# A linear-attention and Fourier-filter kernel on one core: new set-up of the DFT tables, half transposes of q and k, and another order on every engine

## The chip, the core and the metric

The kernel runs on one core of a Trainium2 chip. A core has five engines, each with an instruction queue of its own that is worked off in order: TensorE (PE in the profile; PEld is its weight load), VectorE (DVE), ScalarE (ACT), GpSimd (POOL) and SyncE (SP), which here only issues DMAs. DMAs are issued by SP and POOL and carried out by the core's 16 DMA engines. The metric is the device time of one execution in microseconds (us), lower is better.

## The reference

The inputs are q, k and v (8 batches, 8 heads, 576 positions, 64 wide), a feature map w_phi (64 x 128), a projection w_proj (512 x 1536), a filter (576 x 512) and w_out (512 x 512), all in float32.

```python
def phi(x):
    proj = einsum('bhsd,df->bhsf', x, w_phi)
    proj = proj - max(abs(proj), axis=-1, keepdims=True)
    return concatenate([exp(proj), exp(-proj)], axis=-1)
q_p, k_p = phi(q), phi(k)
kv  = einsum('bhsf,bhsd->bhfd', k_p, v)
z   = sum(k_p, axis=2)
num = einsum('bhsf,bhfd->bhsd', q_p, kv)
den = einsum('bhsf,bhf->bhs', q_p, z)[..., None] + 1e-06
x   = (num / den).transpose(0, 2, 1, 3).reshape(8, 576, 512)

x1, x2, x3 = split(x @ w_proj, 3)
conv = irfft(rfft(x2, axis=1) * rfft(filter_fft, axis=0), n=576, axis=1)
out  = (x1 * conv * x3) @ w_out
```

The Fourier transforms run over the 576 positions.

## The kernel before

**Staging.** The 8 batches go through one pipeline, and about two of them are in work at any time. Positions are held as 9 interleaved groups j, and a batch's 8 heads as four pairs v, so that a batch of q or k is a tile of 128 partitions x 4 pairs x 9 groups x 64 (`qn`, `kn`, `vn`, two or three buffers each). For a batch b the steps are, with the names of the methods that record them:

- `load` brings q, k or v (POOL issues the DMA, which also casts to bf16); `tr` transposes a whole batch of q or k into `qT` or `kT` by one DMA on SP (18 blocks of 128 x 128). For batch 0 `loadh` and `trh` do the same by halves: half X holds the pairs 2X and 2X+1.
- `Pk` and `Qn` multiply a pair of k or q by w_phi on PE into PSUM; `Pkt` and `Qnt` do the ninth group. `maxk`, `maxq`, `maxkt` and `maxqt` take the maximum of absolute values on DVE; `ex` and `exkt` take the exponentials of k on ACT.
- The maximum of q goes into the exponent itself: `mhi` (ACT) and `mlo` (DVE) split it into two bf16 parts in the tile `mh`, `trm` (SP) transposes them into `mT`, and `Pq` (PE) computes the q projection in the other orientation, with a selection matrix `sel` that subtracts the maximum. Then ACT takes the exponentials.
- The maximum of k goes into v: `em` (ACT) and `vs` (POOL) scale v, four `vs` to a batch. `KV` (PE) forms k'v and z, `NE` and `NEt` (PE) the numerators and denominators, `rc` and `xn` (DVE) divide, `trx` and `trxt` (SP) transpose the result into `xT`.
- `X1` and `X3` (PE) project; `fold` and `foldt` (POOL) add and subtract the two halves of the positions into `eo`, which `X2` projects. `F` (PE) is the DFT of x2 with the tables `fwd` and `fwd5`; `m1` (DVE), `m2` and `m3` (POOL) multiply by the filter's spectrum A and B; `I` (PE) is the inverse with the tables `inv`; `Ie`, `Ip`, `Im` and `ym` combine the halves and multiply by x1 x3; `O` (PE) is the last product and `st` (SP) writes.

**The opening.** The DFT tables are computed on the chip. `gen_rows` makes rows of frequencies on one partition, `gen_cols` turns them into columns by 30 matmuls with one output column, `gen_angles` (DVE) multiplies, rounds and subtracts, `gen_sin` (ACT) takes the sines into G and g3, `gen_five` (DVE) makes G5, `gen_fwd` transposes table by table (six DMAs on SP), `gen_inv` (DVE) copies the inverse tables. `gen_sel` (DVE) builds `sel`. `filt_load` brings the filter by 20 DMAs on SP, `filt_fold` (POOL) folds its halves, and `H` (PE) and `H_ev` make A and B.

**What sets the order.** A text, PLAN, lists every step by name and arguments (an @ gives the PSUM bank); `run` calls the methods in that order, with no scheduler behind it:

```python
for word in PLAN.split():
    name, _, bank = word.partition("@")
    self.bank = int(bank) if bank else None
    f, *args = name.split(",")
    getattr(self, f)(*[int(a) if a.isdigit() else a for a in args])
```

So each engine's queue is the PLAN restricted to that engine, and an instruction that waits holds back all that stands behind it on its engine. Buffers come in rings (two of `qT`, `kT` and `xT`), and PSUM has 8 banks.

Of the kernel before, what the change touches and what calls it, by code (L numbers as in the profile page):

```python
# [8 lines left out]
FP32 = mybir.dt.float32  # L9
# [27 lines left out]
w_load,proj,0 rc,0,1@4 xn,0,1@4 ex,k,m,1,2@0 w_load,proj,1 gen_fwd,4 ex,k,p,1,3@6 vs,m,1,1 NE,0,2@2
rc,0,2@2 xn,0,2@2 NEt,0@4 rct,0@4 w_load,proj,2 Qn,1,1@0 maxq,1,1@0 xnt,0,1@4 w_load,proj,3 NE,0,3@2
xnt,0,0@4 trxt,0 Qnt,1@0 em,p,1,1 rc,0,3@2 xn,0,3@2 Pk,1,1@4 ex,k,m,1,3@6 ex,k,m,1,1@4 Qn,1,2@6
maxq,1,2@6 H,2@2 H_ev,ACT,2@2 maxqt,1@0 H,1@3 trx,0,3 vs,p,1,1 Qn,1,0@6 maxq,1,0@6 H_ev,ACT,1@3  # L40
trx,0,1 maxk,1,1@4 Qn,1,3@0 trx,0,2 H_fix H,4@2 H_ev,ACT,4@2 maxq,1,3@0 late foldt,0,1 KV,1,1@6
ex,k,p,1,1@4 Pk,1,0@2 X3t,0@4 trx,0,0 X1t,0@5 X1te,ACT,0@5 foldt,0,0 X2,0,4@0 X3,0,3@5 X1,0,3@1
mhi,1 KVe,DVE,1,1@6 mlo,1 maxk,1,0@2 em,p,1,0 load,k,2 X2e,ACT,0,4@0 em,m,1,0 trm,1 X1,0,2@6
X1e,ACT,0,2@6 fold,0,1 X2,0,2@0 X2e,DVE,0,2@0 load,q,2 tmt,0@4 X2,0,3@7 ex,k,p,1,0@2 load,k,3
X2e,DVE,0,3@7 X1,0,1@6 X1,0,0@4 X1e,DVE,0,0@4 ex,k,m,1,0@2 X1e,ACT,0,1@6 F,0,3@0 fold,0,0 X2,0,1@6
X1e,ACT,0,3@1 tm,0,3@5 X2e,DVE,0,1@6 Pqt,1@2 X2,0,0@1 exqt,m,1@2 exqt,p,1@2 X2e,DVE,0,0@1 F,0,2@6
Fe,DVE,0,2@6 Pq,1,0@4 ex,q,p,1,0@4 ex,q,m,1,0@4 vs,p,1,0 Fe,DVE,0,3@0 vs,m,1,0 F,0,1@1 Fe,DVE,0,1@1
m1,0,3@0 F,0,0@7 Fe,ACT,0,0@7 KV,1,0@2 m1,0,1@1 KVe,ACT,1,0@2 Pq,1,2@4 ex,q,m,1,2@4 ex,q,p,1,2@4
# [846 lines left out]
```

## Time and profile before

| | us |
|---|---|
| median of 3 runs | 376.44 |
| lowest and highest | 373.03, 376.76 |
| the profiled execution, its own time | 378.21 |
| the span that its profile covers | 376.4 |

| engine | busy us | share of the span |
|---|---|---|
| PE | 303.6 | 81% |
| DVE | 273.8 | 73% |
| POOL | 241.2 | 64% |
| ACT | 219.1 | 58% |

The mean granted TensorE clock is 0.951 of full speed. The core read 33.88 MB and wrote 9.44 MB of device memory.

How to read the rows further below: in a timeline row stand the start, the length, the engine, the line of the code (L516), the operation, the tile written and the tiles read (`qT<-qn`), the shapes, how many equal instructions are merged, and in brackets how long the engine sat idle before it and what ended that. In a row by groups the busy time and the mean in ns stand behind the bar, then the idle time before. In the chain of waits stand start, length and who was waited for. SPq is SP's own queue, and its length covers issuing alone, not the transfer.

### The profile page before, as it was taken

The numbers are of one execution on the slowest core, as the hardware profiler recorded it, in microseconds if no ns is written. First come the engines' busy times: TensorE is split into PE (matmuls) and PEld (weight loads), VectorE is DVE, ScalarE is ACT, GpSimd is POOL, SyncE is SP. The second block draws the span as 40 slices with busy tenths as digits, with TensorE's granted clock in tenths as the row PEclk, the third lists the DMA queues.
The fourth block names the chain that finished last, engine by engine and source line by source line (L and its number), as shares of the span: only waits on it lengthen the run. The fifth ranks groups of instructions, "written<-read, shape, count | busy, mean of one in ns | idle before, by whom it ended". The sixth has DMA issues, their size and how long they took to land.

```text
span 376.4 us, 9310 instructions
## 1 busy us (share of the span) xinstructions
PE 303.6 (81%) x3816; PEld 171.1 (45%) x3863; DVE 273.8 (73%) x450; ACT 219.1 (58%) x346; POOL 241.2 (64%) x184
## 2 busy tenths in 40 slices
PE   5230757599939999798699998699897999999993
PEld 5220345335614565355344664247442664564451
DVE  3759678527947899688577799959885798767860
ACT  1153766436736787467456877567674857763342
POOL 5408455296674998687387766783789478856440
PEclk9999988979979999999879999989998999999998
DMA  8998489794998698667949363536706271223226
GB/s 165 179 210 116 78 127 165 118 178 70 147 168 142 108 95 141 140 114 134 186 75 215 73 108 80 99 64 93 152 4 124 51 135 33 60 51 70 57 63 161
DMA packets 82171, 42.82 MB, mean 114 GB/s; under 512 B 63440, under 2 KB 76368, under 8 KB 82128
## 3 DMA queue, kind: packets, MB, share of 16 engines
q1 hardware_dynamic: 68320, 25.97, 38.3%
q0 software_dynamic: 13808, 16.25, 28.4%
q8 instruction: 30, 0.49, 0.5%
q14 instruction: 13, 0.11, 0.1%
HBM read 33.88 MB, written 9.44 MB: 115 GB/s over the span
## 4 chain that ended last, share of the span: by engine, by line
PE 61%; DMA 18%; DVE 11%; issue 4%; SPq 2%; ACT 2%; POOL 0%; DVEq 0%; ACTq 0%; POOLq 0%
PE ps L750 14%; PE ps L719 9%; PE ps L408 8%; PE ps L830 6%; DMA qT<-qn 6%; PE ps L631 5%; DMA xT<-xn 5%; PE ps L652 4%; PE ps L798 4%; DMA kT<-kn 3%; PE ps L543 2%; DMA qn<-in_q_dram 2%; PE ps L537 2%; PE ps L516 2%; DMA mT<-mh 2%
## 5 line engine op out<-in xcount | busy, mean ns | idle before, releaser
L750 PE MATMUL ps<-xT,wproj 128*128 128x512 bf16 x244 | 69.1, 408 | 10.7 <-DMA xT<-xn 9.8
L576 DVE TENSOR_REDUCE mq<-ps 128x8 f32<-128x1024 f32 (+1 forms) x40 | 43.5, 1111 | 22.8 <-PE ps L523 12.1
L818 POOL TENSOR_TENSOR yT<-cv,x1s 128x576 bf16<-128x576 f32 x25 | 32.4, 1315 | 25.6 <-DVE cv L807 19.1
L616 POOL TENSOR_TENSOR vm<-vn,vm 128x1152 bf16<-128x1152 bf16 x16 | 34.4, 2152 | 20.4 <-ACT vm L610 20.4
L737 POOL TENSOR_TENSOR t<-C,B 128x512 bf16<-128x512 bf16 x32 | 36.4, 1154 | 14.5 <-ACT C L636 7.2
L707 POOL TENSOR_TENSOR eo<-xT 128x1024 bf16<-128x1024 bf16 x16 | 35.0, 2196 | 16.1 <-DMA xT<-xn 9.9
L576 DVE TENSOR_REDUCE mk<-ps 128x8 f32<-128x1024 f32 (+1 forms) x40 | 43.7, 1110 | 2.1 <-PE ps L523 0.6
L616 POOL TENSOR_TENSOR vp<-vn,vp 128x1152 bf16<-128x1152 bf16 x16 | 34.4, 2152 | 12.5 <-ACT vp L610 8.8
L408 PE MATMUL ps<-x2n,fwd 128*128 128x512 bf16 (+1 forms) x121 | 38.2, 387 | 4.7 <-DVE x1s L638 3.0
L750 PEld LDWEIGHTS <-wproj 128*128 128x128 bf16 x256 | 23.6, 103 | 39.0 <-issue 14.6
L560 ACT ACTIVATE Ekp<-ps 128x1024 bf16<-128x1024 f32 x32 | 32.8, 1030 | 14.5 <-PE ps L509 13.2
L830 PE MATMUL ps<-wout,yT 128*128 128x512 bf16 x132 | 36.8, 396 | 3.1 <-ACT x1s L636 1.4
L719 PE MATMUL ps<-wproj,eo 128*128 128x512 bf16 x154 | 39.0, 383 | 0.4 <-issue 0.2
L560 ACT ACTIVATE Eqm<-ps 128x1024 bf16<-128x1024 f32 x32 | 32.4, 1025 | 10.0 <-PE ps L543 10.0
L560 ACT ACTIVATE Eqp<-ps 128x1024 bf16<-128x1024 f32 x32 | 32.9, 1028 | 6.9 <-PE ps L543 6.3
L560 ACT ACTIVATE Ekm<-ps 128x1024 bf16<-128x1024 f32 x32 | 32.8, 1029 | 5.3 <-PE ps L509 4.8
L636 ACT CAST x1s<-ps 128x512 bf16<-128x512 f32 (+1 forms) x32 | 17.2, 547 | 29.7 <-PE ps L750 22.0
L745 POOL TENSOR_TENSOR Y<-Y,t 128x1024 bf16<-128x1024 bf16 x14 | 29.7, 2125 | 2.2 <-DVE Y L733 0.9
L733 DVE TENSOR_TENSOR Y<-ps,A 128x512 bf16<-128x512 f32 x40 | 26.6, 682 | 5.4 <-PE ps L408 5.2
L509 PE MATMUL ps<-wphi,kT 64*128 64x128 bf16 x256 | 14.2, 231 | 18.3 <-DVE mk L576 8.8
L807 DVE TENSOR_TENSOR cv<-es,ps 128x288 f32<-128x288 f32 x64 | 25.4, 447 | 4.2 <-ACT es L802 2.3
L798 PE MATMUL ps<-inv,Y 128*128 128x288 bf16 x192 | 28.3, 291 | 0.0
(142 smaller groups left out, 643.6 us busy)
## 6 DMA issues: line engine op xcount, KB each, us to landing
out_dram<-o SPq DMA_DIRECT2D x72, 128.0 KB, 2.4
vn<-in_v_dram POOLq DMA_DIRECT2D x8, 576.0 KB, 7.3
kn<-in_k_dram POOLq DMA_DIRECT2D x7, 576.0 KB, 8.5
qn<-in_q_dram POOLq DMA_DIRECT2D x7, 576.0 KB, 7.5
wproj<-in_moe_w_proj_dram POOLq DMA_DIRECT2D x4, 384.0 KB, 7.0
fl<-in_moe_filter_fft_dram SPq DMA_DIRECT2D x20, 64.0 KB, 5.2
kn<-in_k_dram POOLq DMA_DIRECT2D x2, 288.0 KB, 5.7
qn<-in_q_dram POOLq DMA_DIRECT2D x2, 288.0 KB, 6.8
```

The source lines that it names most:

```text
L408: self.mm(self.pb(0), l, r, start=(i == 0), stop=(i == len(ks) - 1))
L560: self.nc.scalar.activation(e, self.db(), AF.Exp, bias=0.0, scale=1.0 if g == "p" else -1.0)
L576: self.nc.vector.tensor_reduce(out=out, in_=src, axis=AX.X, op=ALU.max, apply_absolute_value=True)
L616: self.nc.gpsimd.tensor_tensor(out=t[:, :, :, 0:64], in0=self.at("vn", b)[:, 2 * X:2 * X + 2], in1=t[:, :, :, 64:65].to_broadcast([128, 2, ...
L707: self.nc.gpsimd.tensor_tensor(out=o, in0=x[:, :, :, 0, :], in1=x[:, :, :, 1, :], op=op)
L719: self.mm(self.pb(0), eo[:, kt, 128 * c:128 * c + 128], w[:, kt, 512:1024], start=(kt == 0), stop=(kt == 3))
L737: self.nc.gpsimd.tensor_tensor(out=self.at("t2", b)[:, t, :], in0=self.at("C", b)[:, t ^ 1, :], in1=self.at("B")[:, t, :], op=ALU.mult)
L745: e.tensor_tensor(out=Y, in0=Y, in1=self.at("t2", b)[:, s, :], op=ALU.add)
L750: self.mm(self.pb(0), w[:, kt, f0 + 128 * m:f0 + 128 * m + 128], x[:, kt, :], start=(kt == 0), stop=(kt == 3))
L798: self.mm(self.pb(e, 0, 288), Y[:, t, 128 * m:128 * m + 128], inv[:, e, i, :], start=(i == 0), stop=(i == 2))
L818: e.tensor_tensor(out=self.at("yT", b)[:, m, 0:SEQ], in0=self.at("cv", 4 * b + m).rearrange("p j h t -> p (j h t)"), in1=self.at("x1s", b) ...
L830: self.mm(self.pb(0), y[:, kt, 128 * j:128 * j + 128], w[:, kt, :], start=(kt == 0), stop=(kt == 3))
```

## The change

The PLAN is written anew from its first word to its last, so that every engine's queue has another order. Around it:

- The columns of frequencies and phases no longer come from matmuls: `gen_cols` makes them on DVE from the bits of the partition number, in some twenty instructions on one to four columns. Seven ACT instructions (`gen_turns`) do the multiplication of the angles, and DVE keeps the rounding and the subtraction, in two parts.
- `gen_five`, `gen_sel` (with the copy `gen_selx`) and `gen_inv` move from DVE to POOL, as do the zeroing of G and G5 and, but for batch 0, `mlo`.
- The six transposes of the tables become two: `gen_fwd` takes all four tables of G at once (12 blocks), `gen_fwd5` both of G5.
- Of the filter, one half is loaded by POOL and one by SP, nine DMAs each instead of ten. `filt_fold` is called in three parts, later in the PLAN.
- `w_proj` is loaded by three blocks of columns (x1, x2, x3) instead of four blocks of rows.
- q and k are transposed by halves in every batch (`trh`), so 32 DMAs take the place of 18.
- A method `warm` and a tile `idle` are added; the PLAN doesn't call `warm`, and `idle` is only zeroed.

The core of the diff:

```diff
 PLAN = """
-gen_phase loadh,k,0,1 loadh,q,0,1 loadh,q,0,0 gen_rows gen_half gen_cols@0 gen_cols_ev@0 gen_angles
-gen_sin loadh,k,0,0 filt_load,SP,0 w_load,phi w_phi trh,q,0,1 Qn,0,3@0 trh,q,0,0 hold,q,0 trh,k,0,0
+w_load,phi w_phi zeros loadh,q,0,0 loadh,q,0,1 gen_rows loadh,k,0,0 trh,q,0,0 Qn,0,0@0 gen_cols,1
+gen_turns,1 gen_cols,0 gen_turns,0 gen_angles,1 Qn,0,1@2 gen_angles,0 maxq,0,0@0 maxq,0,1@2
...
-    def gen_cols(self):
-        for t in range(8):
-            self.mm(self.pb(0, t, t + 1), self.fr[:, t, :], self.one, True, True)
-        for t in range(7):
-            self.mm(self.pb(0, 8 + t, 9 + t), self.ph[:, t, :], self.one, True, True)
...
+        for i in range(3):
+            v.tensor_scalar(out=bit[:, i:i + 1], in0=self.part, scalar1=4 + i, scalar2=1,
+                            op0=ALU.logical_shift_right, op1=ALU.bitwise_and)
...
+    def gen_turns(self, i):
+        cols = self.at("cols")
+        for t in (range(0, 4), range(4, 7))[i]:
+            self.nc.scalar.activation(self.turn[:, t, :], self.sc, AF.Identity,
+                                      bias=cols[:, 8 + t:9 + t], scale=cols[:, t:t + 1])
+
+    def gen_angles(self, i):
+        v = self.nc.vector
+        r = (slice(0, 4), slice(4, 7))[i]
+        t, w = self.turn[:, r, :], self.whole[:, r, :]
+        v.tensor_copy(w, t)
+        v.tensor_tensor(out=t, in0=t, in1=w, op=ALU.subtract)
...
     def gen_five(self):
-        v, m = self.nc.vector, self.at("msk")
+        g, m = self.nc.gpsimd, self.at("msk")
...
-    def gen_fwd(self, t):
-        if t < 4:
-            out, src = self.at("fwd")[:, t, :, :], self.G[:, t, :]
-        else:
-            out, src = self.at("fwd5" if t == 4 else "fwdh"), self.G5[:, t - 4, :]
-        self.nc.sync.dma_start_transpose(out=out, in_=src)
+    def gen_fwd(self):
+        self.nc.sync.dma_start_transpose(
+            out=self.at("fwd").rearrange("p t c x -> p (t c) x"),
+            in_=self.G.rearrange("p t x -> p (t x)"))
+
+    def gen_fwd5(self):
+        self.nc.sync.dma_start_transpose(
+            out=self.at("fwd5").rearrange("p t c x -> p (t c) x"),
+            in_=self.G5.rearrange("p t x -> p (t x)"))
 
     def gen_inv(self):
-        v, inv, m = self.nc.vector, self.at("inv"), self.at("msk")
+        v, inv, m = self.nc.gpsimd, self.at("inv"), self.at("msk")
...
-        q = self.nc.sync if eng == "SP" else self.nc.scalar
+        q = dict(SP=self.nc.sync, ACT=self.nc.scalar, POOL=self.nc.gpsimd)[eng]
...
-            g.dma_start(out=self.at("wproj")[:, kt, :],
-                        in_=self.dram["w_proj"][128 * kt:128 * kt + 128, :])
+            c = slice(512 * kt, 512 * kt + 512)
+            g.dma_start(out=self.at("wproj")[:, :, c],
+                        in_=self.dram["w_proj"][:, c].rearrange("(t p) f -> p t f", p=128))
...
     def gen_sel(self):
-        v, idx = self.nc.vector, self.selidx
+        g, idx = self.nc.gpsimd, self.selidx
...
-    def mlo(self, b):
+    def mlo(self, eng, b):
         m = self.at("mh", b)
-        self.nc.vector.tensor_tensor(out=m[:, :, 1, 0:18], in0=self.at("mq", b),
-                                     in1=m[:, :, 0, 0:18], op=ALU.subtract)
+        e = self.nc.vector if eng == "DVE" else self.nc.gpsimd
+        e.tensor_tensor(out=m[:, :, 1, 0:18], in0=self.at("mq", b),
+                        in1=m[:, :, 0, 0:18], op=ALU.subtract)
```

Where the order moves, place by place. Numbers behind a tile's name tell its buffers apart; L576 before is L598 after (the maxima), L601 is L624 (`mlo`).

**DVE in the opening, from the table subtraction to the maxima of k.** Before:

```order
L576 TENSOR_REDUCE mq_86<-ps 128x2x2
L576 TENSOR_REDUCE mq_86<-ps 128x2x4
L269 MEMSET mh_88 128x64
L269 MEMSET mh_89 128x64
L353 TENSOR_SCALAR G_154<-g_156,msk_74 128x256
```

and, after seven more rows of that kind,

```order
L465 TENSOR_SCALAR selone<-selidx 128x18 x4
L467 TENSOR_TENSOR selone<-selone 128x36
L468 TENSOR_TENSOR selone<-selone 128x18
L469 CAST sel_63<-selone 128x2304
L601 TENSOR_TENSOR mh_88<-mq_86,mh_88 128x2x18
L576 TENSOR_REDUCE mk_84<-ps 128x2x4 x3
```

After:

```order
L352 TENSOR_TENSOR turn<-turn,whole 128x864
L351 CAST whole<-turn 128x1152
L352 TENSOR_TENSOR turn<-turn,whole 128x1152
L598 TENSOR_REDUCE mq_86<-ps 128x2x4 x3
L598 TENSOR_REDUCE mq_86<-ps 128x2x2
L598 TENSOR_REDUCE mq_86<-ps 128x2x4
L598 TENSOR_REDUCE mk_84<-ps 128x2x4
L624 TENSOR_TENSOR mh_88<-mq_86,mh_88 128x2x18
```

Between the last maximum of q (`mq`) and the subtraction into `mh` stood `gen_five` and `gen_sel`; now one maximum of k.

**SP in the opening, up to the transpose of mh.** Before:

```order
L383 DMA fl_203<-in_moe_filter_fft_dram 32x512 x8
L385 DMA fl_203<-in_moe_filter_fft_dram 32x512 x2
L443 DMA phi<-in_w_phi_dram 64x128 x2
L490 DMA_TRANSPOSE qT_81<-qn_75 128x9x128 x2
L490 DMA_TRANSPOSE kT_82<-kn_77 128x9x128 x2
L383 DMA fl_204<-in_moe_filter_fft_dram 32x512 x8
L385 DMA fl_204<-in_moe_filter_fft_dram 32x512 x2
L363 DMA_TRANSPOSE fwd_66<-G 128x3x128 x2
L605 DMA_TRANSPOSE mT_90<-mh_88 128x128
```

After:

```order
L461 DMA phi<-in_w_phi_dram 64x128 x2
L512 DMA_TRANSPOSE qT_81<-qn_75 128x9x128 x2
L512 DMA_TRANSPOSE kT_82<-kn_77 128x9x128 x2
L401 DMA fl_142<-in_moe_filter_fft_dram 32x512 x8
L402 DMA fl_142<-in_moe_filter_fft_dram 32x512
L377 DMA_TRANSPOSE fwd_66<-G 128x12x128
L628 DMA_TRANSPOSE mT_90<-mh_88 128x128
```

Ten filter loads ahead of w_phi and the first transposes are gone from there; the other half of the filter still stands between the transposes of k and `mT`.

**POOL in the opening, up to the first scaling of v (`vp`, L616 before, L639 after) and the filter's folds.** Before:

```order
L474 DMA vn_79<-in_v_dram 128x4x576
L474 DMA qn_76<-in_q_dram 128x4x576
L474 DMA vn_80<-in_v_dram 128x4x576
L390 TENSOR_TENSOR fe<-fl_203,fl_204 128x512
L391 TENSOR_TENSOR fe<-fl_203,fl_204 128x512
L393 TENSOR_TENSOR fe<-fl_203,fl_204 32x512
L390 TENSOR_TENSOR fe<-fl_203,fl_204 128x512
L391 TENSOR_TENSOR fe<-fl_203,fl_204 128x512
L393 TENSOR_TENSOR fe<-fl_203,fl_204 32x512
L616 TENSOR_TENSOR vp_103<-vn_79,vp_103 128x18x64
```

After:

```order
L496 DMA vn_79<-in_v_dram 128x4x576
L491 COPY sel_63<-selone 128x2304
L496 DMA kn_78<-in_k_dram 128x4x576
L496 DMA qn_76<-in_q_dram 128x4x576
L639 TENSOR_TENSOR vp_103<-vn_79,vp_103 128x18x64
L639 TENSOR_TENSOR vm_117<-vn_79,vm_117 128x18x64
L639 TENSOR_TENSOR vp_104<-vn_79,vp_104 128x18x64
L518 COPY junk_71<-qT_81 1x1
L639 TENSOR_TENSOR vm_118<-vn_79,vm_118 128x18x64
L465 DMA wproj_64<-in_moe_w_proj_dram 128x4x512
L410 TENSOR_TENSOR fe<-fl_142,fl_143 32x512 x2
L408 TENSOR_TENSOR fe<-fl_142,fl_143 128x512 x4
```

The folds went behind the four scalings of v, the copy into `sel` came in ahead of them, and ahead of these rows stand now the filter loads, `gen_five` and `gen_sel`.

**SP around the results of batch 2 and q of batch 3.** Before, the whole of q behind the four xT:

```order
L486 DMA_TRANSPOSE kT_82<-kn_77 128x18x128
L690 DMA_TRANSPOSE xT_131<-xn_128 128x4x128 x4
L486 DMA_TRANSPOSE qT_81<-qn_76 128x18x128
L695 DMA_TRANSPOSE xTt_133<-xnt_129 128x2x128
L846 DMA out_dram<-o_805 64x512 x2
```

After, one half ahead of them and one behind:

```order
L512 DMA_TRANSPOSE qT_81<-qn_76 128x9x128
L512 DMA_TRANSPOSE kT_82<-kn_77 128x9x128
L713 DMA_TRANSPOSE xT_131<-xn_128 128x4x128 x4
L869 DMA out_dram<-o_834 64x512 x2
L718 DMA_TRANSPOSE xTt_133<-xnt_129 128x2x128
L512 DMA_TRANSPOSE qT_81<-qn_76 128x9x128
```

A half of q (and one of k of batch 4) now stands ahead of xT on SP, and a write of the output between xT and xTt.

460 lines of the change are left out of this document (235 added, 225 removed).

## The prediction

> **What bounds the kernel now.** I read the page's slices first, then the busy time by stage, the chain that ended last, PE's timeline for its gaps, and last the groups by line for prices. The rows below are the page's busy tenths in 40 slices of 9.4 us.
> ```profile
> PE   5230757599939999798699998699897999999993
> DMA  8998489794998698667949363536706271223226
> ```
> Then the busy time by stage: the stage, its length, busy us of PE, PEld, DVE, ACT and POOL with their counts, the granted clock, the DMA share and GB/s.
> ```profile
> 0.00:40.00 40.00, 12.46 (x112) 10.94 (x113) 26.25 (x53) 12.05 (x16) 17.50 (x25) 1.00 0.97 163
> 40.00:74.50 34.50, 21.86 (x448) 15.03 (x448) 24.05 (x39) 22.28 (x37) 16.84 (x14) 0.89 0.86 127
> 74.50:130.00 55.50, 48.60 (x518) 24.18 (x525) 36.12 (x58) 32.71 (x50) 40.21 (x30) 0.89 0.86 138
> 130.00:220.00 90.00, 81.33 (x1132) 45.65 (x1147) 70.35 (x116) 58.98 (x91) 67.52 (x48) 0.96 0.80 129
> 220.00:370.00 150.00, 139.21 (x1615) 75.29 (x1634) 117.03 (x186) 91.92 (x153) 99.10 (x69) 0.98 0.40 78
> 370.00:376.40 6.40, 0.17 (x1) 0.00 (x0) 0.00 (x0) 1.17 (x2) 0.00 (x0) 0.80 0.68 156
> ```
> There are two kernels here. From 74.5 to 370, PE is busy 269.1 of 295.5 us: it is the bound, and only its gaps can go. Before 74.5 it is busy 34.3 of 74.5 us and waits for a chain through everything else. That chain, start and length:
> ```profile
> 13.77 12.17 DMA kT<-kn
> 26.85 1.82 DVE mq L576 x2
> 35.47 1.25 DVE mh L601
> 36.72 1.15 DVE mk L576
> 48.67 1.17 PE ps L631 x70
> 67.75 6.71 DMA xT<-xn
> 74.52 5.30 PE ps L750 x12
> ```
> L631 is the first KV, L750 at 74.52 the first projection that needs all of batch 0's attention. PE's larger gaps (in brackets, with what ended them):
> ```profile
> 17.87 1.46 PE L516 MATMUL ps<-wphi,qT 64*128 64x128 bf16 x24 [7.02 <-DVE wphi L453]
> 37.91 0.61 PE L509 MATMUL ps<-wphi,kT 64*128 64x128 bf16 x8 [8.80 <-DVE mk L576]
> 109.85 1.46 PE L750 MATMUL ps<-xT,wproj 128*128 128x512 bf16 x3 [4.91 <-DMA xT<-xn]
> 153.24 0.28 PE L523 MATMUL ps<-wphi,qT 64*128 64x128 bf16 x4 [2.12 <-DMA qT<-qn]
> 187.51 0.61 PE L516 MATMUL ps<-wphi,qT 64*128 64x128 bf16 x8 [3.58 <-DMA qT<-qn]
> 229.80 1.89 PE L830 MATMUL ps<-wout,yT 128*128 128x512 bf16 x7 [1.45 <-ACT x1s L636]
> 243.92 1.37 PE L408 MATMUL ps<-x2n,fwd 128*128 128x512 bf16 x3 [3.05 <-DVE x1s L638]
> 269.00 1.46 PE L750 MATMUL ps<-xT,wproj 128*128 128x512 bf16 x6 [1.36 <-DMA xT<-xn]
> 288.09 0.40 PE L543 MATMUL ps<-mT,sel 64*128 64x128 bf16 x8 [1.86 <-DMA mT<-mh]
> ```
> **The change, part by part.** Prices for the opening: timeline and group rows, the landing times of kT, and the spread of the mh subtraction (min, median and max ns).
> ```profile
> 0.74 3.86 SPq L383 DMA_DIRECT2D fl<-in_moe_filter_fft_dram  x8
> 15.40 10.86 SPq L383 DMA_DIRECT2D fl<-in_moe_filter_fft_dram  x8
> 27.42 2.52 SPq L363 DMA_TRANSPOSE fwd<-G  x2
> DMA to landing us min/median/max: 3.3/5.1/12.2
> 28.73 0.52 DVE L353 TENSOR_SCALAR G<-g,msk 128x256 bf16<-128x256 bf16 x1
> 33.18 2.37 DVE L469 CAST sel<-selone 128x2304 bf16<-128x2304 f32 x1
> 41.72 2.15 POOL L616 TENSOR_TENSOR vp<-vn,vp 128x1152 bf16<-128x1152 bf16 x1 [3.72 <-issue]
> 27.90 1.27 POOL L390 TENSOR_TENSOR fe<-fl,fl 128x512 bf16<-128x512 f32 x1 [10.68 <-DMA fl<-in_moe_filter_fft_dram]
> L480 POOL DMA_DIRECT2D kn<-in_k_dram x2 | 1.6, 808 | 0.8 <-POOLq L879 0.8
> L446 POOL DMA_DIRECT2D wproj<-in_moe_w_proj_dram x4 | 2.3, 575 | 0.0
> L713 POOL TENSOR_TENSOR eo<-xTt 128x128 bf16<-128x128 bf16 x16 | 6.6, 425 | 6.1 <-DMA xTt<-xnt 4.9 <-PE ps L509 1.2
> L408 PE MATMUL ps<-fe,fwd 128*128 128x512 bf16 (+1 forms) x10 | 4.3, 497 | 0.7 <-issue 0.3 <-DVE xn L671 0.2
> L601 DVE TENSOR_TENSOR mh<-mq,mh x8: 186/1258/4949, 35.5 to 316.8; 128x36 bf16<-128x36 f32 x8
> 238.32 4.95 DVE L601 TENSOR_TENSOR mh<-mq,mh 128x36 bf16<-128x36 f32 x1 [0.44 <-ACT mh L597]
> 238.94 4.26 POOL L616 TENSOR_TENSOR vp<-vn,vp 128x1152 bf16<-128x1152 bf16 x2
> ```
> *q to PE.* The wphi cast now stands first on DVE, w_phi and the two q halves first on SP, with no filter load ahead. The 7.02 us wait of PE's first projection goes; q's own landing is next, and q's transposes were issued from 8.09 on behind ten filter loads. I take Qn from about 11 instead of 17.87, and the last maxq at about 17 instead of 28.67 (the table angles still take some 4 us of DVE first). Their multiply is now seven ACT instructions, with one more table load; they cost nothing, since ACT has no exp to do until the first Pk, and if that came sooner they would hold it up. The 30 one-column matmuls and 13 memsets on DVE are gone, and their replacement, some twenty tiny DVE instructions, stands in the same place: both hide behind q's landing.
>
> *k's second half.* It took 12.17 us to land because k1, v0, q1, v1 and ten filter loads followed its issue. Now only nine filter loads of POOL stand between, the others behind gen_sel: between 3.3 and 12.2 I take the median 5.1, which puts it at about 17 instead of 25.9.
>
> *The maximum row mT.* Between the last maxq (28.67) and the subtraction (35.47) DVE had gen_five and gen_sel, 6.8 us, and the subtraction 1.25. Both go to POOL. SP now has nine filter loads and one merged 12-block transpose ahead of mT. The loads cost 9 x 0.48 = 4.3 us (first row) to 9 x 1.36 = 12.2 (second row, in which SP also waits for the k transposes); starting at about 12.5 and with the merged transpose at most two issues of the third row (2.5), mT is issued at 19 to 27. I take 23, so Pq at 26 against 39.0.
>
> *POOL.* All that stands ahead of its first vs now: four half loads 4 x 0.81 and two full ones as much each, iotas about 2, nine filter issues at 0.58 to 0.81 (5.2 to 7.3), gen_five, gen_sel and the 2304-column copy. No one-input POOL arithmetic is in the trace. Lower end: DVE's own durations (4 x 0.27 and 4 x 0.22, six at 0.16, 2.37, some 5); upper end: the slope of two-input POOL rows (0.43 for 128 columns, 2.15 for 1152), which gives 11.5. Taken: 8, the middle, since a one-input loop lies between both. Sum from 1.3 us on, with v0's issue: 20 to 29, taken 25, and v0's own landing (about 27) is later still. So vs begins at 27.5, not 41.72; KV, two vs later, at 32 against 48.4. On that stretch ACT's exps and their PSUM banks stay just ahead.
>
> A rule of the Trainium skill speaks against this part. Its page GPSIMD Engine Reference, section Performance versus the Vector engine, calls GpSimd the wrong place for ordinary elementwise work, about 2x slower than VectorE. By it the 6.7 us of DVE rows from 28.73 to 35.47 would be some 13 us on POOL, and the opening 3 us longer than I sum it.
>
> *KV to the first projection* took 74.5 - 48.4 = 26.1 us. New in this stretch: the filter folds, which ran at 27.9 before, now come after the four vs and a w_proj issue, 6 x 1.27 = 7.6 us, and PE's queue has H,1 behind them and ahead of NE,0,3. From vs at 27.5 the folds end at 27.5 + 8.6 + 0.6 + 7.6 = 44.3 plus the hold copy; then PE has some 13 us of work up to the projection (14 filter matmuls at 0.43, some eight Qn and Pk at 0.61, NE and two tail projections), in which xn and its transposes (6.71 to land) hide. That gives 57.5. gen_inv on POOL and the six table transposes, now two on SP, hide there too, and so does w_proj by column blocks, whose first block is the one that the tail projection needs; if the folds came sooner, gen_inv would hold up the eo fold next. The DMA side gives a later time: 0.97 x 40 + 0.86 x 34.5 = 68.5 us of it lay before 74.5, of which v1, one w_proj block and two filter rows move out (0.59 + 0.52 + 0.13 MB by their shapes, at 163 GB/s 7.6 us), leaving 60.9 at a share of 1. I take 60: gain 14.5, bounds 8 (share as before: 66) and 19 (55). KV,1,1, 72 matmuls as in the row at 48.67, is moved behind the projection: +1.3.
>
> *mlo on POOL.* 238.32 and 238.94 end together at 243.2: a 36-column subtraction that can take 0.19 us took 4.95, as long as POOL streamed. That is the gap of 3.05 at 243.92, and it goes: -3. What it costs is one small POOL instruction behind at most a fold of 2.2 us; mT is late next, so the 1.86 at 288.09 stays. The same page, section Specifications, lists the SBUF interface as shared with VectorE instructions that read two SBUF inputs; the 186 against 4949 ns agree.
>
> *Halves of q and k.* The same blocks in two issues; a half lets Qn and Pk of two blocks start before the second. In batch 3 and 4 q's halves now stand before or between the xT transposes. The gaps 2.12 and 3.58 are bounded by 0 and 5.7; I take -4.
>
> *New order.* 4.91 at 109.85 lies in a DMA-dense stage and stays. 1.45 and 1.36 may stay or move; for new gaps of the same kind I put +2 (0 to 8). The end keeps its 6.4 us after the last matmul.
>
> Sum: 376.4 - 14.5 + 1.3 - 3 - 4 + 2 = 358.2 of span. The profiled run took 378.21 with 376.4 of span, so 1.8 more: **360.0**. The median shown, 376.44, lies 1.8 below that run.
>
> **Rivals.** *POOL paces the opening:* the upper prices and filter issues as slow as SP's 1.36 put vs at 34 and the projection at 66: 376.4 - 8.5 + 1.3 - 5 + 1.8 = 366. For it: POOL gets the most added work, and no row prices it. Against: v0's landing covers part. The page's rule above points the same way. *DMA gives it back*: share 0.86 to 0.97 through 130 us; the projection at 66, the 4.91 gap grows and the q gaps stay: 376.4 - 8.5 + 1.3 - 3 + 1 + 1.8 = 369. Against: shares in shorter stages pass 1. *It doesn't do what it says*: H,1 in PE's queue waits for folds, the merged table transpose or filter rows until about 60, the projection comes at 72 and the later gaps only move: 376.4 - 2.5 + 1.3 + 1.8 = 377. *Slower: SP's queue.* Halves now stand ahead of xT on SP and wait there for their loads or buffers; before, a whole transpose waited so:
> ```profile
> SPq L486 <- PE ps L798: 19.9, 4, 7.3
> ```
> That is 5.0 us each. Where xT is held as long in a batch, PE has nothing else. Five such batches cost 25: 385. From a little over four (20.2 us) it is slower by over 1%; below that the opening pays.
>
> **How the numbers follow.** Forecast 0.64 (own range 349 to 367), POOL 0.12, DMA 0.10, no change 0.08, slower 0.06. The range takes the bounds of the opening (8 to 19) and of the later gaps: low 376.4 - 19 + 1.3 - 3 - 5.7 - 2.8 (1.45 and 1.36) + 1.8 = 349; high 371, past the DMA case; the last two rivals and a tail below 349 are left out. About 1%, some 3.8 us, is what a measurement of this kernel can tell from no change: faster (under 372.7) 0.84, within 0.09, slower 0.07.
>
> **What would show it.** First Qn by 12 us, Pq by 28, first KV by 34, first full projection by 63; POOL's first vs at 25 to 30; no gap of PE ended by DVE while it subtracts mh; no gap over 1 us ended by qT in batches 3 and 4. Wrong if POOL reaches vs after 35, if folds end after 50, or if PE's waits for xT grow in later batches with SP's queue standing on a qT or kT transpose.

## The result and the profile after

| | before | after |
|---|---|---|
| median, us | 375.80 (4 runs, 373.03 to 376.76) | 351.01 (4 runs, 348.15 to 357.69) |
| the profiled execution, its own time | 378.21 | 352.66 |
| the span that its profile covers | 376.4 | 350.6 |
| mean granted TensorE clock | 0.951 | 0.987 |

The ratio is 0.933, 95% interval 0.923 to 0.943: the changed kernel is faster by 7%. That lies inside the range, 9 us below the predicted 360. Runs of one program spread by a few per cent, so each ratio is formed from a kernel's faster runs, while the profiles of e5, e7, e9, e10 and e11 below fell in slower ones. The 25.8 us between the two spans aren't where the prediction had put them. Line numbers of the changed kernel run 17 to 23 higher: L773 is the first projection (L750 before), L654 is KV, L565 the product with `mT`, L425 the DFT.

The first view of after is the page's slices, PE and DMA; its 40 slices are 8.8 us each.

```profile
PE   0040567799789999999999999799989999999982
DMA  7999999999979999685793577474975601431236
```

The second is the busy time by stage, cut at the first full projection as before was: length, busy us of PE, PEld, DVE, ACT and POOL, granted clock, DMA share, GB/s.

```profile
0.00:66.65 66.65, 25.53 (x455) 18.50 (x457) 33.59 (x67) 37.83 (x55) 45.88 (x67) 0.99 1.12 147
66.65:130.00 63.35, 58.83 (x814) 32.32 (x823) 49.44 (x81) 47.20 (x70) 51.25 (x38) 0.96 1.04 155
130.00:220.00 90.00, 87.58 (x1158) 48.17 (x1170) 77.85 (x119) 64.08 (x109) 72.55 (x55) 1.00 0.72 127
220.00:344.00 124.00, 118.19 (x1371) 63.85 (x1386) 97.21 (x163) 74.22 (x121) 82.18 (x60) 1.00 0.45 85
```

The opening shrank by 7.9 us (74.52 to 66.65, where the chain that ended last puts the first projection; PE's own row of it starts at 66.46); the prediction had 14.5. From the first projection to the last matmul, PE was busy 269.1 of 295.5 us before, idle for 26.4; now it is busy 264.6 of 277.4, idle for 12.8. So the later stage gave 18 us: 13.6 of PE's waits, and 4.5 of busy time, at a clock of 0.96 to 1.00 where it was 0.89 to 0.98. The prediction had 3.7 there (3 + 4 - 2 - 1.3). Two errors of opposite sign met in a good total, which is luck: the opening gave a little less than its lower bound of 8, and the later 18 us are more than its own bounds allowed (3 + 5.7 + 2.8 - 1.3 = 10.2).

The third view is the timeline of the opening, PE's rows first and then SP's and POOL's. In brackets stand the idle time and what ended it.

```profile
16.93 1.03 PE L538 MATMUL ps<-wphi,qT 64*128 64x128 bf16 x16 [16.93 <-DMA qT<-qn]
36.93 0.61 PE L565 MATMUL ps<-mT,sel 64*128 64x128 bf16 x8 [8.80 <-DMA mT<-mh]
41.34 0.62 PE L654 MATMUL ps<-vp,Ekp 64*128 64x65 bf16 x16 [2.09 <-ACT Ekm L582]
5.51 7.17 SPq L512 DMA_TRANSPOSE qT<-qn  x2
25.69 1.40 SPq L628 DMA_TRANSPOSE mT<-mh  x1
20.62 0.85 POOL L496 DMA_DIRECT2D vn<-in_v_dram  x1
23.52 0.76 POOL L496 DMA_DIRECT2D kn<-in_k_dram  x1
24.27 0.75 POOL L496 DMA_DIRECT2D qn<-in_q_dram  x1
29.02 2.14 POOL L639 TENSOR_TENSOR vp<-vn,vp 128x1152 bf16<-128x1152 bf16 x1 [4.00 <-ACT vp L633]
```

What is to be seen: q's transposes were issued at 5.51, and PE could use them at 16.93; `mT` was issued at 25.69, and PE could use it at 36.93. Each took about 11 us to land. In flight with `mT` were three loads of 1.2 MB as read, k and q of batch 1 just ahead of it, and in SP's own queue the merged transpose of the tables, issued at 23.34.

After 66.65 PE has only two waits over 1 us left, where before had seven of 1.4 to 4.9:

```profile
222.57 1.77 PE L425 MATMUL ps<-x2n,fwd 128*128 128x512 bf16 x5 [2.09 <-DVE x1s L661]
256.46 0.40 PE L565 MATMUL ps<-mT,sel 64*128 64x128 bf16 x8 [1.38 <-DMA mT<-mh]
```

### The profile page after: what moved, and what is told of

It reads as the page before. It is cut to its first block, busy times and chain, and to the rows that moved or that the text cites. A ratio compares the mean times of both kernels' runs of the same rounds, so it can differ in the third digit from the quotient of the medians.

```text
span 350.6 us, 9276 instructions
## 1 busy us (share of the span) xinstructions
PE 290.4 (83%) x3789; PEld 162.8 (46%) x3833; DVE 258.1 (74%) x426; ACT 224.5 (64%) x355; POOL 251.9 (72%) x217
## 4 chain that ended last, share of the span: by engine, by line
PE 66%; DMA 12%; DVE 10%; POOL 4%; issue 4%; ACT 3%; SPq 0%; DVEq 0%; POOLq 0%; ACTq 0%
PE ps L773 15%; PE ps L425 9%; PE ps L742 8%; PE ps L853 7%; PE ps L821 6%; PE ps L654 5%; DMA mT<-mh 5%; PE ps L675 4%; DMA qT<-qn 3%; DVE yT L841 2%; PE ps L565 2%; PE ps L780 2%; PE ps L559 2%; DVE mq L598 2%; DMA xTt<-xnt 2%
## 5 line engine op out<-in xcount | busy, mean ns | idle before, releaser
L773 PE MATMUL ps<-xT,wproj 128*128 128x512 bf16 x239 | 64.9, 391 | 1.6 <-DVE xnt L706 0.3
L598 DVE TENSOR_REDUCE mq<-ps 128x8 f32<-128x1024 f32 (+1 forms) x40 | 43.2, 1110 | 9.3 <-PE ps L538 8.9
L639 POOL TENSOR_TENSOR vp<-vn,vp 128x1152 bf16<-128x1152 bf16 x16 | 34.6, 2163 | 16.3 <-ACT vp L633 15.4
L598 DVE TENSOR_REDUCE mk<-ps 128x8 f32<-128x1024 f32 (+1 forms) x40 | 44.0, 1112 | 2.5 <-ACT Ekp L582 1.4
L582 ACT ACTIVATE Eqm<-ps 128x1024 bf16<-128x1024 f32 x32 | 32.6, 1030 | 15.3 <-PE ps L565 14.5
L425 PE MATMUL ps<-x2n,fwd 128*128 128x512 bf16 (+1 forms) x123 | 38.2, 383 | 3.6 <-DVE x1s L661 2.1
L841 POOL TENSOR_TENSOR yT<-cv,x1s 128x576 bf16<-128x576 f32 x22 | 27.9, 1278 | 15.6 <-DVE cv L830 14.1
L730 POOL TENSOR_TENSOR eo<-xT 128x1024 bf16<-128x1024 bf16 x16 | 34.0, 2132 | 5.1 <-DMA xT<-xn 5.1
L853 PE MATMUL ps<-wout,yT 128*128 128x512 bf16 x138 | 35.8, 380 | 2.2 <-DVE x1s L661 0.9
L773 PEld LDWEIGHTS <-wproj 128*128 128x128 bf16 x256 | 23.2, 100 | 26.7 <-issue 3.9
L639 POOL TENSOR_TENSOR vm<-vn,vm 128x1152 bf16<-128x1152 bf16 x16 | 34.4, 2152 | 1.5 <-ACT vm L633 1.4
L659 ACT COPY o<-ps 128x512 f32<-128x512 f32 x29 | 17.0, 588 | 27.4 <-PE ps L853 18.8
L538 PE MATMUL ps<-wphi,qT 64*128 64x128 bf16 x256 | 13.2, 229 | 20.2 <-DMA qT<-qn 16.9
```

The costliest lines, as they stand in the source:

```text
L425: self.mm(self.pb(0), l, r, start=(i == 0), stop=(i == len(ks) - 1))
L582: self.nc.scalar.activation(e, self.db(), AF.Exp, bias=0.0, scale=1.0 if g == "p" else -1.0)
L598: self.nc.vector.tensor_reduce(out=out, in_=src, axis=AX.X, op=ALU.max, apply_absolute_value=True)
L639: self.nc.gpsimd.tensor_tensor(out=t[:, :, :, 0:64], in0=self.at("vn", b)[:, 2 * X:2 * X + 2], in1=t[:, :, :, 64:65].to_broadcast([128, 2, ...
L730: self.nc.gpsimd.tensor_tensor(out=o, in0=x[:, :, :, 0, :], in1=x[:, :, :, 1, :], op=op)
L773: self.mm(self.pb(0), w[:, kt, f0 + 128 * m:f0 + 128 * m + 128], x[:, kt, :], start=(kt == 0), stop=(kt == 3))
```

## The experiments

Two questions stood open: what made the later 18 us, and why the opening gave only 8. All times are medians; a ratio is to the kernel before on the same chip, with its 95% interval. e7 and e9 have no interval, so their range stands instead. The steps in the diffs are words of PLAN.

**e1, the new opening with the old order behind it.** The changed kernel's code and PLAN up to `late` (and the steps that empty the PSUM banks then open); behind that the order of before, whole transposes, `mlo` on DVE.

```diff
-late maxk,1,3@0 X1te,ACT,0@2 tmt,0@3 X1,0,2@5 foldt,0,1 mhi,1 w_load,proj,1 em,p,1,0 X1e,DVE,0,2@5
+late w_load,proj,1 maxk,1,3@0 X1te,ACT,0@2 tmt,0@3 ex,k,p,1,2@6 ex,k,m,1,3@0 ex,k,m,1,2@6 X1e,DVE,0,3@4
+load,v,1 em,m,1,1 vs,m,1,1 em,p,1,1 vs,p,1,1 foldt,0,1 KV,1,1@6 foldt,0,0 X2,0,4@0 X3,0,3@5
...
```

> The changed kernel's opening (its order up to the point at which the set-up ends), followed by the order of before for everything else: whole transposes of q and k where they are not yet issued, mlo on DVE. The traces put the first full projection at 74.52 us before and at 66.65 after, and from there to the end 301.9 and 284.0 us. Theory A (the opening and the later stage are separate, the opening is worth its 7.9 us): 375.8 - 8 = 368, with a projection at about 66 and 300 us behind it. Rival B (the later gain is a consequence of the better opening: batch 1 is further ahead when the steady stage begins): 352 to 356. Rival C (the opening's gain is lost again when the old order sets in): 375.

Measured: 378.67 us, ratio 1.0105 (1.006 to 1.015). PE and POOL in the timeline where the old order sets in, and then three stretches of 4 us in the columns of the table above:

```profile
63.24 1.02 PE L764 MATMUL ps<-xT,wproj 128*128 128x512 bf16 x4 [0.16 <-DVE mq L589]
73.50 0.62 PE L645 MATMUL ps<-vp,Ekp 64*128 64x65 bf16 x16 [9.24 <-POOL vp L630]
60.98 0.75 POOL L487 DMA_DIRECT2D vn<-in_v_dram  x1
69.20 2.15 POOL L630 TENSOR_TENSOR vm<-vn,vm 128x1152 bf16<-128x1152 bf16 x1 [7.47 <-DMA vn<-in_v_dram]
```

```profile
68.00:72.00 4.00, 0.00 (x0) 0.00 (x0) 0.00 (x0) 0.00 (x0) 2.80 (x2) 0.50 0.05 9
72.00:76.00 4.00, 2.50 (x73) 2.13 (x73) 0.22 (x1) 0.00 (x0) 4.00 (x4) 0.50 0.01 4
76.00:80.00 4.00, 4.00 (x19) 1.82 (x18) 0.81 (x3) 1.16 (x2) 3.99 (x5) 0.94 0.53 68
```

The projection begins at 63.24, 11 us before that of the kernel before, and then most of the lead is lost in one place: the old order wants `KV,1,1` at once, and the new opening loads v of batch 1 only at 60.98. PE waits 9.24 us and then works at half clock until 76; at the wait for xT that stood at 109.85 before, e1 is at 108.31. The opening's gain is lost with an order that doesn't expect its state, as rival C had it. Another way of joining the two, with v loaded sooner, was not tried.

**e2, the old opening with the new order behind it.** The code of before, `mlo` with an engine as argument, `late` followed by the changed kernel's steps.

```diff
-late foldt,0,1 KV,1,1@6 ex,k,p,1,1@4 Pk,1,0@2 X3t,0@4 trx,0,0 X1t,0@5 X1te,ACT,0@5 foldt,0,0 X2,0,4@0
+late ex,k,p,1,1@4 Pk,1,0@2 ex,k,p,1,0@2 ex,k,m,1,0@2 maxk,1,0@2 trx,0,0 X3t,0@3 load,k,2 em,m,1,0 X1t,0@2
...
```

> The opening of before (its order and its way to make the tables, up to the end of the set-up), followed by the changed kernel's order: half transposes from there on, mlo on GpSimd from batch 1 on. Theory A: the later 17.9 us come from the later order and what goes with it, so 375.8 - 18 = 358, projection at 74 to 75 and 284 us behind it. Rival B (the opening makes the later gain): 370 to 376.

Measured: 358.23 us, ratio 0.952 (0.946 to 0.958), 17 us below before. In its profile the full projections begin at 71.4 and the span ends at 357.3: 285.9 us behind it, against 283.9 in after and 301.9 before. Theory A held: the later gain doesn't come from the opening.

**e5, e6 and e12, the two code changes of the later stage in the old order.** e5 moves `mlo` to GpSimd (in the kernel that ran, that of batch 0 too), e6 writes each whole transpose as two halves in one place, e12 does both, with batch 0's `mlo` left on DVE.

```diff
-Pq,3,3@4 ex,q,m,3,3@4 trx,3,0 tr,q,4 ex,q,p,3,3@4
+Pq,3,3@4 ex,q,m,3,3@4 trx,3,0 trh,q,4,0 trh,q,4,1 ex,q,p,3,3@4
-em,m,4,0 mlo,4 trm,4
+em,m,4,0 mlo,POOL,4 trm,4
...
```

> The kernel before with one edit: the subtraction mlo of batches 1 to 7 on GpSimd instead of DVE, in the same places of the order. e3_mlo_dve lost about 18 us when the changed kernel did the reverse. Theory P (the engine counts only with the new order, whose matmuls on mT stand close behind): the old order gains what the prediction put, the 3.05 us gap: 371 to 374. Rival Q (mlo on DVE was the bound of the old order too): 357 to 362. Rival R (on GpSimd it now waits behind scalings and folds of about 2.1 us each that stood behind it before, and mT comes later): 378 to 384.

> The kernel before with one edit: every whole transpose of q and k as two halves, one right behind the other. Theory H (halves as such let Qn and Pk begin sooner and remove the two gaps ended by qT, 5.7 us): 369 to 372. Rival N (halves in one place are no better, since the second half lands when the whole did): 374 to 377.

> The kernel before, its order kept, with both parts that the later stage gained in code: mlo on GpSimd in batches 1 to 7 (batch 0 on DVE) and every q and k transposed as two halves in one place. e2_rest, the same opening with the changed kernel's later order, took 358.2. Theory O (the later order makes the gain, and mlo and the halves are what it needs): 367 to 373, as e5_old_mlo_pool and e6_old_halves one by one add up to. Rival C (the two code changes together make it, whatever the order): 357 to 362.

Measured: e5 370.06 us, ratio 0.985 (0.967 to 1.002); e6 378.12, ratio 1.0145 (1.002 to 1.027); e12 370.48, ratio 0.988 (0.980 to 0.995), 6.6 us below the kernel before on its chip. e5 came out a microsecond below what theory P gave, with an interval that reaches no change; e6 is no faster, as rival N said; e12 lies where theory O put it. The four longest waits of PE in e12 behind the first projections:

```profile
102.73 1.52 PE L746 MATMUL ps<-xT,wproj 128*128 128x512 bf16 x3 [5.70 <-DMA xT<-xn]
147.65 0.23 PE L518 MATMUL ps<-wphi,qT 64*128 64x128 bf16 x2 [2.27 <-DMA qT<-qn]
182.48 0.61 PE L511 MATMUL ps<-wphi,qT 64*128 64x128 bf16 x8 [3.39 <-DMA qT<-qn]
241.47 0.40 PE L538 MATMUL ps<-mT,sel 64*128 64x128 bf16 x8 [1.65 <-DMA mT<-mh]
```

The wait of 3.05 us for DVE is gone, a smaller one for `mT` stands at its place, and both gaps ended by qT (2.12 and 3.58 before) are still there: a half right behind a half lands no sooner. e12 and e2 have the same code and, but for batch 1's transposes in halves, the same opening; they differ in the later order, the places of the halves included: 370.5 against 358.2. With both code changes present that order is worth 10 to 13 us (17.0 against 6.6 us below the kernel before, each on its own chip; the ratios give 13.5, with an uncertainty of some 4), and rival C falls.

What the order does can be read at the first of the old waits, the 4.91 us at 109.85. The last transposes of xT of batch 1 before (the first row) and after, and PE's first product from them after:

```profile
99.21 4.12 SPq L690 DMA_TRANSPOSE xT<-xn  x3
93.62 2.53 SPq L713 DMA_TRANSPOSE xT<-xn  x2
99.12 0.58 PE L773 MATMUL ps<-xT,wproj 128*128 128x512 bf16 x1 [0.20 <-DVE mq L598]
```

Before, SP had issued the last of them at 103.3 and PE wanted them at 104.94; after, at 96.15 and 99.12. The four of the batch took 2.4 to 10.4 us to land before and 2.5 to 5.7 after, so both the distance and the landing changed. How the 10 to 13 us divide between the two, the runs don't show.

**e3 and e11, `mlo` back on DVE in the new order.** e3 in the same place, e11 right behind `mhi`.

```diff
-X2,1,0@6 X2e,ACT,1,4@7 X2,1,1@7 mlo,POOL,2 trm,2
+X2,1,0@6 X2e,ACT,1,4@7 X2,1,1@7 mlo,DVE,2 trm,2
...
```

and in e11, where some twenty steps lie between the two places

```diff
-mhi,2 X3,0,3@6 X1,1,1@7 X1e,ACT,1,1@7
+mhi,2 mlo,DVE,2 X3,0,3@6 X1,1,1@7 X1e,ACT,1,1@7
...
-X2,1,0@6 X2e,ACT,1,4@7 X2,1,1@7 mlo,POOL,2 trm,2
+X2,1,0@6 X2e,ACT,1,4@7 X2,1,1@7 trm,2
...
```

> The changed kernel with the subtraction mlo on DVE in every batch, in the same places. Theory M (mlo beside GpSimd's scaling of v is what held PE): 3 us or more are lost per long mlo that PE waits for, so 354 to 360, and a gap of PE ended by x1s or mT behind a DVE mlo of some 5 us. Rival O (the new order's longer distances hide it): 350 to 352, though single mlo rows on DVE take 1 to 5 us again.

> The changed kernel with mlo on DVE in every batch as in e3_mlo_dve, but directly behind mhi instead of in mlo's own place, so that up to four DVE operations no longer stand ahead of it. Theory W (e3_mlo_dve lost 18 us because mlo stood behind other work in DVE's queue): 352 to 357. Rival V (it is DVE itself: mlo runs 1 to 5 us long beside GpSimd, and DVE now also waits for mhi on ACT): 363 or more.

Measured: e3 368.95 us, ratio 0.983 (0.975 to 0.990); e11 359.01, ratio 0.962 (0.955 to 0.968). The spread of `mlo` in after, in e3 and in e11 (min, median and max ns, first and last start), and how long PE waited for it by way of `mT` (us, times):

```profile
L624 POOL TENSOR_TENSOR mh<-mq,mh x7: 243/250/257, 67.3 to 286.1; 128x36 bf16<-128x36 f32 x7
...
  PE ps L565: 10.2, 2
```

```profile
L616 DVE TENSOR_TENSOR mh<-mq,mh x8: 188/780/2858, 24.1 to 300.6; 128x36 bf16<-128x36 f32 x8
...
  PE ps L557: 23.8, 6
```

```profile
L616 DVE TENSOR_TENSOR mh<-mq,mh x8: 186/960/2800, 24.3 to 295.4; 128x36 bf16<-128x36 f32 x8
...
  PE ps L557: 17.3, 6
```

About 8 to 10 us of each figure (8.80 in after, 7.77 in e3, 10.28 in e11) are the first wait, in the opening; behind it 1.4, 16.0 and 7.0 us are left. On GpSimd `mlo` takes 250 ns each time. On DVE it takes up to 2.9 us, and in mlo's place it also stands behind other DVE work. e3 lost more than either of its expectations had; e11 lies between its two. Of the 19 us that e3 lost (0.983 against 0.933 of 376), some 8 were the place in DVE's queue, and some 11, with an uncertainty of about 5, were left with `mlo` on DVE even at the earliest place. The longer waits for `mT` cover most of e3's loss and half of e11's; the rest wasn't traced.

**e4 and e7, whole transposes in the new order.** Each whole q and k from batch 1 on at the place of its first half (e4) or its second (e7).

```diff
-trh,q,4,0 NE,3,0@2 X3,2,0@5 xnt,3,0@6
+tr,q,4 NE,3,0@2 X3,2,0@5 xnt,3,0@6
...
-Qn,4,1@6 trh,q,4,1 tmt,2@4 trx,3,0 maxq,4,1@6
+Qn,4,1@6 tmt,2@4 trx,3,0 maxq,4,1@6
...
```

> The changed kernel with q and k of batch 1 on transposed whole, each at the place of its first half. Theory H (the halves remove the waits for qT, 2.12 and 3.58 us before): 355 to 357, with such gaps back. Rival O (the order, which issues them earlier, does it): 350 to 352. Rival S (a whole transpose stands ahead of xT on SP and holds it, in several batches): 358 or more.

> The changed kernel with q and k of batch 1 on transposed whole, each at the place of its second half (e4_whole had them at the first half's place and took 378.8, with SP standing up to 10 us on a load or a buffer). Theory S (e4_whole lost by SP's waits for loads and buffers, which the later place has not): 352 to 358. Rival H (a whole transpose is what costs: half of q and k comes too late at any place): 365 or more, with gaps of PE ended by qT or kT.

Measured: e4 378.84 us, ratio 1.010 (1.006 to 1.014); e7 371.42 us (361.9 to 375.9). SP's waits in e4, one of PE's there, and two of PE's in e7:

```profile
SPq L500 <- DMA kn<-in_k_dram: 10.3, 1, 10.3
SPq L500 <- PE ps L523: 14.3, 2, 9.9
286.92 0.61 PE L551 MATMUL ps<-qT,wphi 64*128 64x512 bf16 x2 [5.52 <-DMA qT<-qn]
```

```profile
96.51 0.61 PE L529 MATMUL ps<-wphi,qT 64*128 64x128 bf16 x8 [4.26 <-DMA qT<-qn]
155.47 0.40 PE L536 MATMUL ps<-wphi,kT 64*128 64x128 bf16 x4 [5.07 <-DMA kT<-kn]
```

At the early place SP stands up to 10 us on a load that isn't there or a buffer that PE still reads, as rival S said; at the late place Qn and Pk wait, as rival H said. Against the changed kernel's median, 24.8 us below the kernel before, e4 (3.6 above) loses some 28 us and e7 (5.3 below) some 20; by e7's shortest run, 361.9, it is 15, and with its wide range e7's size is uncertain. Here the halves count, at these two places: whether a whole transpose would do at a third was not tried. In the changed kernel SP stands on loads too, up to 8.6 us behind the opening, but neither of PE's two waits over 1 us there is ended by qT or kT. Why the gap at 286.92, the longest of four such, stands at Pq, whose q was transposed before, the trace doesn't show.

**e8, e9 and e10, the opening's transpose of mh.** e8 loads k and q of batch 1 behind the first two scalings of v. e10 moves SP's filter loads and the table transpose behind `trm` as well, and spreads the two loads. e9 is the changed kernel again, beside e10.

```diff
-load,k,1 load,q,1 vs,p,0,0 vs,m,0,0 KV,0,0@2
+vs,p,0,0 vs,m,0,0 load,k,1 load,q,1 KV,0,0@2
```

and in e10

```diff
-gen_sel mlo,DVE,0 filt_load,SP,0 maxk,0,2@6 load,v,0
+gen_sel mlo,DVE,0 maxk,0,2@6 load,v,0
...
-trm,0 gen_selx
+trm,0 filt_load,SP,0 gen_fwd gen_selx
...
+vs,p,0,0 load,k,1 vs,m,0,0 KV,0,0@2
...
+vs,m,0,1 load,q,1 KV,0,1@6
```

> The changed kernel with the loads of k and q of batch 1 moved behind GpSimd's first two scalings of v (from 23.5 us to about 33). Theory D (mT takes 11.2 us to land because these loads and v's share the DMA engines with it): mT lands 4 to 8 us sooner, Pq at 29 to 33 instead of 36.9, the first full projection up to 4 us sooner unless batch 1 is now late: 347 to 351. Rival E (mT waits for something else, the filter loads or the merged table transpose ahead of it in SP's queue): Pq stays at 36 to 37 and the time at 351 to 355, since the loads come later for nothing.

> The changed kernel unaltered, to stand beside e10_fill_the_hole on one chip: 349 to 353, ratio to before 0.925 to 0.94.

> The changed kernel with SP's nine filter loads and the table transpose moved behind the transpose of mh, and k and q of batch 1 loaded behind GpSimd's first and fourth scaling of v. e8_loads_late had mT land 7.7 us sooner, but left the DMA engines nearly idle from 30 to 35 us (share 0.14) and lost the gain to k of batch 1. Theory D (the opening is paced by the DMA engines, at a share over 1 from 5 to 66 us, so a gain on the path stays only if no DMA time is wasted): the filter fills the hole, first KV at 33 to 35, first full projection at 61 to 64 and 346 to 349. Rival F (k of batch 1 is late again, or the filter now holds up the folds and PE's filter matmuls): 351 to 355.

Measured: e8 352.91 us, ratio 0.946 (0.927 to 0.965); e9 353.69 (346.3 to 363.2); e10 356.94, ratio 0.955 (0.947 to 0.963). The transpose and PE in e8's timeline, and then three of its stretches:

```profile
25.14 1.55 SPq L620 DMA_TRANSPOSE mT<-mh  x1
29.27 0.61 PE L557 MATMUL ps<-mT,sel 64*128 64x128 bf16 x8 [1.89 <-DMA mT<-mh]
33.68 0.62 PE L646 MATMUL ps<-vp,Ekp 64*128 64x65 bf16 x16 [2.09 <-ACT Ekm L574]
47.97 0.61 PE L523 MATMUL ps<-wphi,kT 64*128 64x128 bf16 x8 [7.07 <-DMA kT<-kn]
```

```profile
30.00:35.00 5.00, 2.91 (x70) 2.32 (x68) 0.00 (x0) 4.58 (x6) 5.00 (x5) 1.00 0.14 11
48.00:52.00 4.00, 2.91 (x38) 2.21 (x39) 2.12 (x3) 2.08 (x3) 3.84 (x6) 0.50 1.15 186
52.00:56.00 4.00, 3.78 (x36) 2.06 (x36) 2.04 (x6) 1.92 (x5) 0.00 (x0) 0.50 1.24 207
```

and the same two views of e10

```profile
34.12 0.62 PE L646 MATMUL ps<-vp,Ekp 64*128 64x65 bf16 x16 [2.03 <-ACT Ekm L574]
52.06 0.61 PE L523 MATMUL ps<-wphi,kT 64*128 64x128 bf16 x8 [10.51 <-DMA kT<-kn]
```

```profile
25.00:30.00 5.00, 1.37 (x18) 0.76 (x14) 3.71 (x4) 4.76 (x11) 0.89 (x1) 1.00 0.39 93
52.00:56.00 4.00, 2.91 (x36) 2.21 (x37) 2.11 (x3) 1.98 (x3) 0.51 (x1) 1.00 1.53 75
```

With the loads out of the way `mT` lands in 4 us instead of 11, and KV begins at 33.7 instead of 41.3. e8's theory D was right about the cause of the 11 us. But nothing came of it: k of batch 1 is then late, and PE waits 7 and 10.5 us for it. In e8's profile the first full projection begins at 65.77, where it was; in e10's at 75.48. e8 is no different from the changed kernel within its interval. e10, meant to use the hole, still had a share of 0.39 there and was no faster; its rival F showed, at a time 2 us above F's range, and e9 came out a microsecond above its own. No version tried beats the changed kernel.

That the DMA engines set the pace of the opening is not shown. Share times length is 74.6 us of DMA time in after (1.12 x 66.65) and 61.2 in e8 (0.93 x 65.77), at the same 147 GB/s and with the projection in the same place, so the share is no fixed amount of work. What bounds the opening stays open.

## Why the prediction was right in total and wrong in its parts

- *q to PE*, predicted at 11 us with the last maxq at 17: measured 16.93, with the DVE run of maxima ending at 22.8. The filter loads ahead of q's transposes are gone as said, but the landing of the transposes, 11.4 us, had no row in the sum; the step looked at issues only. What slowed it (k's loads and nine filter loads run beside it) was not tried.
- *The maximum row mT*: the issue was predicted at 23 and came at 25.69; Pq, three microseconds later in the prediction, came 11.2 later. This is the step that failed in the opening: the landing of a small transpose was taken as short, and e8 shows that the two loads make the difference between 4 and 11 us. Yet that alone wasn't the opening's bound, since e8 gained nothing by it.
- *POOL*: vs predicted at 27.5, measured 29.02, as its wait for ACT's scaling factors ended; these came last and not v's landing, and POOL was free at 25.0, as taken (the bounds of that sum come out at 19 and 28, not 20 and 29). `gen_five`, `gen_sel` and the copy cost 8.9 us against 8 taken; the rows:

```profile
L371 POOL TENSOR_SCALAR G<-g,msk 128x256 bf16<-128x256 bf16 x4 | 3.7, 917 | 0.5 <-ACT g L363 0.5
L491 POOL COPY sel<-selone 128x2304 bf16<-128x2304 bf16 x1 | 2.1, 2125 | 0.0
```

 The middle between the two bounds came close partly by luck: the upper one, 11.5, doesn't follow from the rows it names, since a line through 0.43 us for 128 columns and 2.15 for 1152 gives 9.2 for the same instructions, so that 8.9 lies near the top. The Trainium skill's rule in GPSIMD Engine Reference, section Performance versus the Vector engine, that such work is about 2x slower there, doesn't hold for the copy, 2.13 us here, reading bf16, against 2.37 for DVE's cast of the same tile from fp32; `gen_five`'s 128x256 rows are slower than by it, 0.92 us against 0.27 for most of DVE's.
- *KV to the first projection*: 60 was taken, between 66 ("share as before") and 55. The four vs, `gen_inv` and the folds ran as summed, the folds ending at 46.0 against 44.3. The stretch itself took 25.3 us (41.34 to 66.65) against 28 in the sum (32 to 60), so by the sum the loss lies ahead of KV, though in e8 an earlier KV brought the projection no nearer. The projection came at 66.65 in the profiled run, and at 65.2 in e9's: the lower bound of the gain. The DMA side had given 60.9 at a share of 1, from bytes that move out. The bytes did fall, from 10.9 MB to 9.8 by rate and length, but the share came out at 1.12 where before had 0.92, and the DMA time rose from 68.5 us to 74.6: a share of 1 was no limit, and DMA time couldn't be counted off by bytes.
- *mlo on POOL* (3 us) and *halves* (4 us): in the old order the two together gave 6.6 (e12), close to the 7, but mostly through `mlo`, as far as e5's wide interval shows; the halves by themselves gained nothing (e6). Their real worth is in the new order, which loses about 19 us without the one (e3) and 15 to 28 without the other, at the two places tried (e7, e4). The prediction priced them one by one in the order of before.
- *New order*, put as a loss of 2 us with bounds of 0 and 8: a gain of 10 to 13 (e2 against e12). This is the largest error. "4.91 at 109.85 lies in a DMA-dense stage and stays" was wrong: it is gone, and so are the 1.45 and 1.36. The step put at a loss what was the main gain: the order wasn't read for how far a product stands from what it waits for; only the gaps' releasers were.
- *The rivals*: DMA giving it back was right about the opening and wrong about the later stage. In the changed kernel no wait of PE over 1 us behind the opening is ended by xT, so SP's queue cost nothing there; e4, where a whole transpose stands early, is as slow as that rival's mechanism would make it, though its long waits are ended by qT and not by xT. What the changed profile was to show held for POOL's vs, for `mlo`, and for the qT gaps of batches 3 and 4; not for Qn, Pq, KV or the projection.

The wait of 2.09 at 222.57 that is left isn't `mlo`'s. DVE multiplies `yT` just ahead of it, while POOL scales v:

```profile
217.38 4.35 DVE L841 TENSOR_TENSOR yT<-cv,x1s 128x576 bf16<-128x576 f32 x1
216.84 2.17 POOL L639 TENSOR_TENSOR vp<-vn,vp 128x1152 bf16<-128x1152 bf16 x1
218.95 2.16 POOL L639 TENSOR_TENSOR vm<-vn,vm 128x1152 bf16<-128x1152 bf16 x1
```

The same multiplication takes 0.76 us in the median of ten. That GpSimd holds it up is read from the overlap and was not tried.

## What to carry to other kernels

A change of order is to be priced by how long before its use each operand is now made, place by place, not by the gaps of the old trace; and a part of it (an engine for a small step, a split transfer) is worth what the new order does with it, which can be several times its price in the old one. A transfer's landing under load has to be summed, not its issue alone; and taking a load out of one product's way can make the next product wait instead, as in e8 and e10, with a lost clock on top.

## What the runs showed of the hardware that wasn't expected

- A DMA transpose of one 128 x 128 block took 11.2 us to land with k's and q's loads of 1.2 MB in flight and about 4 with these two held back (e8), against a median of 3.5 over its eight uses in after.
- A wait of PE costs more than its length. After 9.24 us of it in e1 the granted clock was 0.50 until 76 us, and after 7.07 us in e8 it was 0.50 in the rows from 48 to 56. The Trainium skill, TensorE: Matmul & The Clock Gate, section What's actually happening, puts such a fall to half rate after an idle window of about 3.4 us. e1 and e8 agree. e10's row from 52 to 56 reads 1.00 after a wait of 10.51 us, but its products don't bear that out: the sixteen `ps<-KVs` from 53.91 on start 0.055 us apart, as e8's do at 0.50 from 49.82 on, where those of after start 0.031 apart from 50.43 on. So e10's products ran at about half rate as well, and the clock column doesn't show it. It doesn't in after's opening either: from 44.39 on they start 0.055 apart, in a stage listed at 0.99.
- A two-input operation of DVE can take 2.8 to 5 us instead of 0.19 (`mlo`), or 4.35 instead of 0.76 (`yT`), and in the two cases whose rows are shown (4.95 and 4.35) POOL was streaming v for nearly as long, through two instructions.
